# Eight PSUM banks assigned step by step, score blocks of three key chunks, and reordered first loads in an attention and feed-forward kernel

## The chip, the cores and the metric

The kernel runs on one core of one Trainium2 chip. TensorE does the matmuls and writes them to PSUM, which the kernel uses as eight banks; ACT, DVE and POOL are the other engines that compute. The metric is device microseconds of one execution, median over several, with the range beside it. Each timed execution also lists its mean granted TensorE clock (1.0 is full speed). A profile is one execution taken by the hardware profiler. Its span, from first to last instruction, is some 2 us shorter than the time of the same execution.

## The reference

```python
def _attn_ref(q, k, v, tau):            # 8 x 12 heads, 448 positions, 64 wide
    q_n = q / (norm(q) + 1e-06);  k_n = k / (norm(k) + 1e-06)
    scores = q_n @ k_n.T / tau
    attn = exp(scores - max);  attn /= sum(attn) + 1e-09
    return attn @ v
def _moe_ref(x, w1, w2, w3, w_out):     # x: 3584 x 768
    return ((x @ w1) * (x @ w2)) @ w3 @ w_out
```

## The kernel before

A scheduler in the kernel (class `Plan`) knows all steps, an assumed duration for each and the rings of buffers. It places the steps on the engines greedily in assumed time and then emits them, so the order on every engine is fixed when the kernel is built. Two heads make a pair; 48 pairs go through transposes (`tr`), scores, exponentials, the product with V (`av`), a transpose back (`tb`), and then the products of the feed-forward part ("fills": `a`, `b`, output groups, and at first the product w3 x w_out). Fills have the lowest rank and fill TensorE wherever attention leaves room. The parts that the change touches:

```python
psS = tile_pool(name="psS", bufs=2, space=PSUM)   # scores: 2 x 2 banks
psA = tile_pool(name="psA", bufs=1, space=PSUM)   # av: 1 bank
psT = tile_pool(name="psT", bufs=1, space=PSUM)   # tr and tb: 1 bank
psM = tile_pool(name="psM", bufs=2, space=PSUM)   # fills: 2 banks
...
def scores(pp, half):
    ...
    for c in (2 * half, 2 * half + 1):            # two key chunks in one block
        sc = psS.tile([128, 2, 512], FP32, tag="sc", name="sc")
        for hh in range(2):                       # two heads, 64 rows each, side by side
            kq = qks[pp][64 * hh:64 * hh + 64].rearrange("p t s -> p (t s)")
            nc.tensor.matmul(sc[:, hh, :S], kq[:, c * P:c * P + 128], kq[:, S:],
                             start=True, stop=True)
...
loads = ["w30", "wo0", "q0", "k0", "w31", "v0", "w32", "q1", "k1", "wo1", "w33",
         "w34", "v1", "q2", "wo2", "k2", "w10", "w20", "v2"]     # then q3 k3 v3 ...
...
for n in range(60):                               # warm-up matmuls while nothing else can run
    add(f"warm{n}", [("PE", 0.78 if n < 4 else 0.39)], 10000 + n, ..., until=11.0)
```

## Time and profile before

| what | value | how to read it |
|---|---|---|
| time, before the prediction | 401.64 us (401.2 to 402.2, 3 executions) | |
| span of the profile | 399.0 us | |
| TensorE busy | 98% | busy is not peak: gaps inside the stream count as busy |
| ACT, POOL, DVE busy | 62%, 62%, 55% | averages; POOL is at 91 to 96% from 40 to 240 us |
| mean granted clock | 0.995 | one fall to half speed near 16 us |

### The profile page before, as it was taken

To read this page: it belongs to the slowest core of one execution; us is meant where nothing else is said; L and a number is where in the kernel's file an instruction comes from. 1 tells how busy PE (TensorE), PEld (TensorE's weight loads), DVE (VectorE), ACT (ScalarE), POOL (GpSimd) and SP (SyncE) were. 2 spreads that over 40 slices of the span, in tenths; PEclk is the share of its full clock that TensorE was granted. 3 is DMA by queue.
4 is the path that set the end of the run, shared out by engine and by line. 5 is a ranking of instruction groups with operands and counts; after the bars stand their busy time and mean duration, and the time that the engine had idled before them with its cause. 6 is when DMAs were issued, how large, how long until landed. Compare 5 with 4: busy or idle time off the path is not lost.

```text
span 399.0 us, 9513 instructions
## 1 busy us (share of the span) xinstructions
PE 389.2 (98%) x4006; PEld 231.5 (58%) x4006; DVE 218.2 (55%) x490; ACT 247.7 (62%) x402; POOL 247.2 (62%) x260
## 2 busy tenths in 40 slices
PE   8799999999999999999999999999999999999996
PEld 4578665556555666555655556654665467555553
DVE  4986745685666946576566686643454244220210
ACT  3887667656777777678777777677467733223222
POOL 8779698899999999999999999960100000000000
PEclk9899999999999999999999999999999999999999
DMA  9999999073863758528485256200111004103005
GB/s 164 200 204 209 212 197 153 5 102 81 144 73 41 99 112 152 73 34 106 74 151 72 35 69 116 81 2 0 41 41 41 2 2 112 47 0 111 10 5 156
DMA packets 43691, 35.18 MB, mean 88 GB/s; under 512 B 3968, under 2 KB 37632, under 8 KB 43648
## 3 DMA queue, kind: packets, MB, share of 16 engines
q0 software_dynamic: 38368, 23.11, 42.3%
q1 hardware_dynamic: 4784, 11.07, 9.6%
q8 instruction: 31, 0.51, 0.5%
q10 hardware_dynamic: 496, 0.40, 0.3%
q14 instruction: 12, 0.10, 0.1%
HBM read 46.66 MB, written 11.01 MB: 145 GB/s over the span
## 4 chain that ended last, share of the span: by engine, by line
PE 74%; POOL 19%; DVE 3%; issue 2%; ACT 0%; ACTq 0%; POOLq 0%; DVEq 0%
PE ps_b L337 15%; PE ps_a L337 15%; PE ps_o L337 14%; PE ps_av L302 10%; PE sc L287 8%; POOL sq L231 8%; POOL nrm L257 8%; PE ps_w L337 5%; PE ps_tr L270 4%; PE ps_tb L324 2%; POOL v_sb L216 2%; PE ps_warm L437 2%; POOL raw L200 2%; DVE ss L237 1%; PE ps_w L350 1%
## 5 line engine op out<-in xcount | busy, mean ns | idle before, releaser
L293 ACT ACTIVATE expT<-sc 112x896 bf16<-112x896 f32 x192 | 165.9, 914 | 46.5 <-PE sc L287 46.4
L337 PEld LDWEIGHTS <-w_sb 128*128 128x128 bf16 x768 | 71.0, 98 | 60.3 <-issue 3.0
L257 POOL TENSOR_TENSOR nrm<-raw,rn 112x512 bf16<-112x512 bf16 x90 | 90.7, 1035 | 8.9 <-ACT rn L252 8.8
L231 POOL TENSOR_TENSOR sq<-raw 112x512 bf16<-112x512 bf16 x87 | 87.9, 1039 | 0.3
L337 PE MATMUL ps_a<-xT,w_sb 128*128 128x448 bf16 x384 | 83.1, 353 | 0.0
L337 PE MATMUL ps_b<-xT,w_sb 128*128 128x448 bf16 x384 | 83.0, 352 | 0.0
L337 PE MATMUL ps_o<-w_sb,abT 128*128 128x384 bf16 (+2 forms) x456 | 79.9, 323 | 0.0
L383 DVE TENSOR_TENSOR abT<-a_sb,ps_b 128x448 bf16<-128x448 bf16 x64 | 39.6, 619 | 69.2 <-PE ps_b L337 67.0
L237 DVE TENSOR_REDUCE ss<-sq 112x8 f32<-112x512 bf16 x96 | 63.4, 678 | 13.3 <-POOL sq L231 13.1
L302 PEld LDWEIGHTS <-expT 112*128 112x128 bf16 x1536 | 58.1, 98 | 19.0 <-issue 11.5
L302 PE MATMUL ps_av<-v_sb,expT 112*128 112x65 bf16 x1536 | 65.4, 194 | 0.0
L372 ACT CAST a_sb<-ps_a 128x448 bf16<-128x448 f32 x64 | 34.1, 532 | 45.4 <-PE ps_a L337 43.9
L337 PEld LDWEIGHTS <-abT 128*128 128x128 bf16 x456 | 41.8, 98 | 25.8 <-issue 2.2
L287 PE MATMUL sc<-qkT 64*128 64x448 bf16 x384 | 53.0, 354 | 0.0
L343 ACT COPY out_sb<-ps_o 128x384 f32<-128x384 f32 (+2 forms) x46 | 21.7, 471 | 40.1 <-PE ps_o L337 39.5
L315 DVE TENSOR_TENSOR osd<-ps_av,rs 128x256 bf16<-128x256 f32 x96 | 40.7, 424 | 3.3
L314 DVE RECIPROCAL rs<-ps_av 128x4 f32<-128x4 f32 x96 | 17.2, 179 | 42.1 <-PE ps_av L302 40.7
L278 DVE COPY qkT<-ps_tr 128x896 bf16<-128x896 bf16 x48 | 29.7, 619 | 6.7 <-PE ps_tr L270 6.6
L216 POOL COPY v_sb<-vraw 112x1536 bf16<-112x1536 bf16 x16 | 23.4, 1460 | 15.5 <-PE ps_av L302 15.5
L270 PE MATMUL ps_tr<-ident,nrm 112*128 112x112 bf16 x384 | 27.6, 215 | 1.2 <-DVE nrm L257 1.1
L270 PEld LDWEIGHTS <-nrm 112*128 112x128 bf16 x384 | 20.5, 98 | 13.6 <-issue 7.4
L331 DVE COPY xT<-ps_tb 128x448 bf16<-128x448 bf16 x48 | 18.5, 386 | 15.3 <-PE ps_tb L324 14.7
(37 smaller groups left out, 209.3 us busy)
## 6 DMA issues: line engine op xcount, KB each, us to landing
vraw<-in_v_dram POOLq DMA_DIRECT2D x16, 336.0 KB, 6.2
raw<-in_q_dram POOLq DMA_DIRECT2D x15, 336.0 KB, 5.1
raw<-in_k_dram POOLq DMA_DIRECT2D x15, 336.0 KB, 6.3
w_sb<-in_moe_w_dram POOLq DMA_DIRECT2D x2, 1536.0 KB, 26.3
out_dram<-out_sb SPq DMA_DIRECT2D x7, 336.0 KB, 2.8
out_dram<-out_sb SPq DMA_DIRECT2D x8, 288.0 KB, 2.9
out_dram<-out_sb SPq DMA_DIRECT2D x8, 240.0 KB, 2.8
w_sb<-in_moe_w_dram POOLq DMA_DIRECT2D x3, 512.0 KB, 15.4
```

Of the source, the lines that this page charges most:

```text
L216: nc.gpsimd.tensor_copy(v_tiles[g % NV][:, :, :, :D], vraws.pop(g))
L231: eng.tensor_mul(o, x, x)
L237: nc.vector.reduce_sum(sss[g][:, t, 2 * i:2 * i + 2, :], sqs.pop((g, i, t)), axis=AX.X)
L257: eng.tensor_mul(nrms[g][:, i, t].rearrange("p j h d -> p h j d"), raw_of(g, t, i), rns[g][:, t, 2 * i:2 * i + 2].to_broadcast([P, 2, NJ, D]))
L270: nc.tensor.transpose(ps[:, 1 - t, j * P:(j + 1) * P], n[:, i, t, j].rearrange("p h d -> p (h d)"), ident[:P, :P])
L287: nc.tensor.matmul(sc[:, hh, :S], kq[:, c * P:c * P + 128], kq[:, S:], start=True, stop=True)
L293: nc.scalar.activation(exps[pp][:, c], scs.pop((pp, c))[:P, :, :S], ACT.Exp, scale=1.0 / float(tau))
L302: nc.tensor.matmul(ps[:, m, :], exps[pp][:, c, hh, q0:q0 + 128], vt[:, 2 * i + hh, c, :], start=(c == 0), stop=(c == NJ - 1))
L315: nc.vector.tensor_mul(osds[pp][:, :, hh, :], ps[:, :, :D], rs.to_broadcast([128, NJ, D]))
L337: nc.tensor.matmul(o, l, r, start=(i == 0), stop=(i == len(pairs) - 1))
L372: nc.scalar.copy(a_sbs[b, fo], pms.pop(("a", b, fo))[:, :S])
L383: nc.vector.tensor_mul(abts[b // 2][:, fo, c0:c0 + S], a_sbs.pop((b, fo)), pms.pop(("b", b, fo))[:, :S])
```

## The change

Its intent is to take the banks out of fixed pools: one PSUM tile of eight banks is indexed, and the scheduler gives each TensorE step a free bank when it places it. Scores get three slots of two banks, so that a block can hold three key chunks and may reach from one pair into the next. The other short tiles may use the same six banks between score blocks. The first loads are reordered and those of the fourth group moved up. From the diff, with cuts and some comments added:

```diff
-    psS = ctx.enter_context(tc.tile_pool(name="psS", bufs=2, space=PSUM))
-    (psA, psT, psM likewise)
+    ps_all = psum.tile([128, 8, 512], FP32, name="ps")
...
-    loads = ["w30", "wo0", "q0", "k0", "w31", "v0", "w32", "q1", "k1", "wo1", "w33",
-             "w34", "v1", "q2", "wo2", "k2", "w10", "w20", "v2"]
+    loads = ["wo0", "q0", "k0", "w30", "w31", "w32", "v0", "q1", "k1", "wo1", "q2",
+             "w33", "v1", "w34", "wo2", "q3", "k2", "w10", "k3", "v3", "w20", "v2"]
...
+    PM = [(n,) for n in (7, 6, 5, 4, 3, 2)]          # banks for fills
+    SHORT = [(n,) for n in range(6)]                 # banks for tr, av, tb
+    while at < len(all_chunks):
+        n = 2 if all_chunks[at][0] < NFIRST else 3   # NFIRST = 6
+        blocks.append((at, all_chunks[at:at + n]))
+        at += n
...
-                     [("DVE", 0.1 + n * 0.00105), ("ACT", 0.2 + n * 0.00065)],
+                     [("DVE", 0.1 + n * 0.00105)] +
+                     ([("ACT", 0.2 + n * 0.00065)] if n > 128 else []),   # last output copy
```

More of the change, by code (lines that the diff above doesn't have):

```diff
@@ L38, in __init__ @@
         self.taken = {r: [] for r in rings}
+        self.owner, self.bank, self.reads = [None] * 8, {}, {}
     def given(self, name, time):
@@ L42, in given, with add @@
         self.where[name] = "DMA"
-    def add(self, name, on, rank, emit, after=(), takes=(), holds=(), kb=0, later=None,
-            until=None, slack=0.0, port=False, lead=None):
+    def add(self, name, on, rank, emit, after=(), takes=(), holds=(), reads=(), kb=0, later=None,
+            until=None, slack=0.0, port=False, lead=None, banks=()):
         self.steps[name] = dict(on=on, rank=rank, emit=emit, after=list(after), later=later,
-                                takes=list(takes), kb=kb, until=until, slack=slack, port=port, lead=lead or {})
+                                takes=list(takes), kb=kb, until=until, slack=slack, port=port, lead=lead or {},
+                                banks=banks)
+        for user, part in reads:
+            self.reads.setdefault(user, []).append((name, part))
         for key in holds:
@@ L76, in earliest @@
             t = max(t, self.port["POOL" if eng == "DVE" else "DVE"])
+        if st["banks"]:
+            when = [(self.opens(group, eng), group) for group in st["banks"]]
+            when = [x for x in when if x[0] is not None]
+            if not when:
+                return None
+            t = max(t, min(x[0] for x in when))
+            st["pick"] = next(group for at, group in when if at <= t)
         if st["kb"] and len(self.lanes) >= self.LANES:
@@ L79, in earliest, with readers, opens @@
         return None if st["until"] is not None and t > st["until"] else t
+    def readers(self, name, b):
+        return [r for r, x in self.reads.get(name, ()) if x is None or b in self.bank[name][x]]
+    def opens(self, group, eng):
+        at = [self.gone(self.owner[b], eng) if self.owner[b] else 0.0 for b in group]
+        return None if None in at else max(at)
     def order(self):
@@ L119, in order @@
                 self.taken[r].append(key)
+            if st["banks"]:
+                self.bank[n] = st["pick"]
+                for b in st["pick"]:
+                    self.owner[b] = ("bank", n, b)
+                    self.holders.setdefault(("bank", n, b), self.readers(n, b))
             for u in users.get(n, ()):
@@ L158 @@
     NP = B * NPAIR
+    NFIRST = 6
     QT = (0, 128, 256, S - 128)
@@ L173 @@
     opool = ctx.enter_context(tc.tile_pool(name="opool", bufs=3))
-    psS = ctx.enter_context(tc.tile_pool(name="psS", bufs=2, space=PSUM))
-    psA = ctx.enter_context(tc.tile_pool(name="psA", bufs=1, space=PSUM))
-    psT = ctx.enter_context(tc.tile_pool(name="psT", bufs=1, space=PSUM))
-    psM = ctx.enter_context(tc.tile_pool(name="psM", bufs=2, space=PSUM))
+    psum = ctx.enter_context(tc.tile_pool(name="psum", bufs=1, space=PSUM))
+    ps_all = psum.tile([128, 8, 512], FP32, name="ps")
     w1_sb = wpool.tile([128, KO1, DF], BF16, name="w1_sb")
@@ L262, with full, half @@
     qks, exps, osds, xts, pst, scs, pav = {}, {}, {}, {}, {}, {}, {}
+    def full(name):
+        return ps_all[:, plan.bank[name][0]]
+    def half(name):
+        return full(name).bitcast(BF16).rearrange("p (t n) -> p t n", t=2)
     def tr(pp):
@@ L266, in tr @@
         n = nrms[g]
-        ps = psT.tile([128, 2, 512], BF16, tag="tr", name="ps_tr")
+        ps = half(f"tr{pp}")
         for t in range(2):
@@ L278, in tr_copy, with scores @@
         nc.vector.tensor_copy(qks[pp], pst.pop(pp)[:, :, :S])
-    def scores(pp, half):
-        if half == 0:
-            exps[pp] = exp_pool.tile([P, NJ, 2, S], BF16, tag="exp", name="expT")
-        for c in (2 * half, 2 * half + 1):
-            sc = psS.tile([128, 2, 512], FP32, tag="sc", name="sc")
+    def scores(name, chunks):
+        for n, (pp, c) in enumerate(chunks):
+            if c == 0:
+                exps[pp] = exp_pool.tile([P, NJ, 2, S], BF16, tag="exp", name="expT")
+            b = plan.bank[name][2 * n]
+            sc = scs[pp, c] = ps_all[:, b:b + 2]
             for hh in range(2):
@@ L289, in scores @@
                     start=True, stop=True)
-            scs[pp, c] = sc
     def exp(pp, c):
@@ L298, in av @@
         vt = v_tiles[g % NV]
-        ps = psA.tile([128, NJ, D + 1], FP32, tag="av", name="ps_av")
+        ps = full(f"av{pp}.{hh}")[:, :NJ * (D + 1)].rearrange("p (m d) -> p m d", m=NJ)
         for m, q0 in enumerate(QT):
@@ L321, in trback @@
             xts[b] = xpool.tile([128, NPAIR, S], BF16, tag="xT", name="xT")
-        ps = psT.tile([128, 2, 512], BF16, tag="tr", name="ps_tb")
+        ps = half(f"tb{pp}")
         for m, q0 in enumerate(QT):
@@ L347, in w3t @@
     def w3t(fo):
-        ps = pms["w3t", fo] = psM.tile([128, KO2, 128], BF16, tag="pm", name="ps_w3")
+        ps = pms["w3t", fo] = half(f"w3t{fo}").rearrange("p t (k n) -> p (t k) n", n=128)
         for go in range(KO2):
@@ L355, in w34 @@
     def w34(fo, part, cols):
-        ps = pms["w34", fo, part] = psM.tile([128, 512], FP32, tag="pm", name="ps_w34")
+        ps = pms["w34", fo, part] = full(f"w34.{fo}.{part}")
         mm_group([(w3t_sb[:, go, fo * 128:(fo + 1) * 128], wo_sb[:, go, cols])
@@ L365, in a_group @@
     def a_group(b, fo):
-        ps = pms["a", b, fo] = psM.tile([128, 512], FP32, tag="pm", name="ps_a")
+        ps = pms["a", b, fo] = full(f"a{b}.{fo}")
         mm_group([(w1_sb[:, ko, fo * 128:(fo + 1) * 128], xts[b][:, ko, :])
@@ L374, in b_group @@
     def b_group(b, fo):
-        ps = pms["b", b, fo] = psM.tile([128, 512], FP32, tag="pm", name="ps_b")
+        ps = pms["b", b, fo] = full(f"b{b}.{fo}")
         mm_group([(w2_sb[:, ko, fo * 128:(fo + 1) * 128], xts[b][:, ko, :])
@@ L407, in out_group @@
     def out_group(bb, ch, cols):
-        ps = pms["o", bb, ch, cols.start] = psM.tile([128, 512], FP32, tag="pm", name="ps_o")
+        ps = pms["o", bb, ch, cols.start] = full(f"o{bb}.{ch}.{cols.start}")
         mm_group([(abts[bb][:, fo, ch * 128:(ch + 1) * 128], w34_sb[:, fo, cols])
@@ L432, with warm @@
     ident = const.tile([128, 128], BF16)
-    def warm():
-        ps = psM.tile([128, 512], FP32, tag="pm", name="ps_warm")
+    def warm(n):
+        ps = full(f"warm{n}")
         for _ in range(2):
@@ L444 @@
     plan = Plan(
-        rings=dict(sc=2, av=1, tr=1, pm=2, raw=3, vraw=2, vt=NV, sq=6, nrm=3, qkT=2, osd=2,
+        rings=dict(raw=3, vraw=2, vt=NV, sq=6, nrm=3, qkT=2, osd=2,
                    exp=3, xT=2, a_sb=KO2, big=1, out_sb=3),
@@ L458 @@
         weights[f"w3{n}"] = (w3_sb, moe_w3, part, every)
-    loads = ["w30", "wo0", "q0", "k0", "w31", "v0", "w32", "q1", "k1", "wo1", "w33",
-             "w34", "v1", "q2", "wo2", "k2", "w10", "w20", "v2"]
-    for g in range(3, NG):
+    loads = ["wo0", "q0", "k0", "w30", "w31", "w32", "v0", "q1", "k1", "wo1", "q2",
+             "w33", "v1", "w34", "wo2", "q3", "k2", "w10", "k3", "v3", "w20", "v2"]
+    for g in range(4, NG):
         loads += [f"q{g}", f"k{g}", f"v{g}"]
@@ L536 @@
             [f"v{g}", "ones"], [("vt", ("vt", g))], [("vraw", g)],
-            slack=0.8 if g > 0 else 0.0)
+            slack=0.8 if g > 0 else 0.0, port=True)
+    PM = [(n,) for n in (7, 6, 5, 4, 3, 2)]
+    SHORT = [(n,) for n in range(6)]
+    all_chunks = [(p, c) for p in range(NP) for c in range(NJ)]
+    blocks, at = [], 0
+    while at < len(all_chunks):
+        n = 2 if all_chunks[at][0] < NFIRST else 3
+        blocks.append((at, all_chunks[at:at + n]))
+        at += n
+    for nb, (at, ch) in enumerate(blocks):
+        ps = sorted({p for p, _ in ch})
+        slots = [b for n in range(len(ch)) for b in (2 * ((at + n) % 3), 2 * ((at + n) % 3) + 1)]
+        add(f"sc{nb}", [("PE", 0.205 + 0.187 * len(ch))], ch[0][0] + 0.25 * ch[0][1] - 1,
+            lambda e, nb=nb, ch=ch: scores(f"sc{nb}", ch),
+            [f"ev{p}" for p in ps] + ([f"sc{nb - 1}"] if nb else []),
+            [("exp", ("exp", p)) for p, c in ch if c == 0], [("qkT", p) for p in ps],
+            banks=[tuple(slots)])
+        for n, (p, c) in enumerate(ch):
+            add(f"exp{p}.{c}", [("ACT", 0.82)], p + 0.25 * c - 1,
+                lambda e, p=p, c=c: exp(p, c),
+                [f"sc{nb}"] + ([f"exp{p}.{c - 1}"] if c else [f"exp{p - 1}.{NJ - 1}"] if p else []),
+                reads=[(f"sc{nb}", slice(2 * n, 2 * n + 2))],
+                lead={f"sc{nb}": 0.187 * (len(ch) - 1 - n)})
     for p in range(NP):
@@ L544 @@
             [f"scale{p}.0", f"scale{p}.1", "ident"] + ([f"tr{p - 1}"] if last else []),
-            [("tr", ("tr", p)), ("qkT", ("qkT", p))], [("nrm", g)],
-            slack=0.3 if g > 2 else 0.0)
+            [("qkT", ("qkT", p))], [("nrm", g)],
+            slack=0.3 if g > 2 else 0.0, banks=SHORT)
         add(f"ev{p}", [("DVE", 0.54)], p - 1.1, lambda e, p=p: tr_copy(p), [f"tr{p}"],
-            holds=[("tr", p)])
-        for h in range(2):
-            add(f"sc{p}.{h}", [("PE", 0.58)], p + 0.5 * h - 1, lambda e, p=p, h=h: scores(p, h),
-                [f"ev{p}"] + ([f"sc{p}.0"] if h else [f"sc{p - 1}.1"] if last else []),
-                [("sc", ("sc", p, 2 * h)), ("sc", ("sc", p, 2 * h + 1))]
-                + ([] if h else [("exp", ("exp", p))]), [("qkT", p)])
-            for c in (2 * h, 2 * h + 1):
-                add(f"exp{p}.{c}", [("ACT", 0.82)], p + 0.25 * c - 1,
-                    lambda e, p=p, c=c: exp(p, c),
-                    [f"sc{p}.{h}"] + ([f"exp{p}.{c - 1}"] if c else []), holds=[("sc", p, c)])
+            reads=[(f"tr{p}", None)])
         for h in range(2):
@@ L561 @@
                 + ([f"av{p}.0"] if h else [f"av{p - 1}.1"] if last else []),
-                [("av", ("av", p, h))] + ([] if h else [("osd", ("osd", p))]),
-                [("exp", p), ("vt", g)])
+                [] if h else [("osd", ("osd", p))], [("exp", p), ("vt", g)], banks=SHORT)
             add(f"an{p}.{h}", [("DVE", 0.62)], p + 0.5 * h - 0.5,
-                lambda e, p=p, h=h: av_norm(p, h), [f"av{p}.{h}"], holds=[("av", p, h)])
+                lambda e, p=p, h=h: av_norm(p, h), [f"av{p}.{h}"], reads=[(f"av{p}.{h}", None)])
         add(f"tb{p}", [("PE", 0.235)], p + 1, lambda e, p=p: trback(p),
             [f"an{p}.0", f"an{p}.1"] + ([f"tb{p - 1}"] if last else []),
-            [("tr", ("tb", p))] + ([] if blk else [("xT", ("xT", b))]), [("osd", p)])
+            [] if blk else [("xT", ("xT", b))], [("osd", p)], banks=SHORT)
         add(f"xt{p}", [("DVE", 0.31)], p - 0.2, lambda e, p=p: tb_copy(p), [f"tb{p}"],
-            holds=[("tb", p)])
+            reads=[(f"tb{p}", None)])
     line = []
@@ L582, in fill @@
     def fill(nm, cost, em, after, on, em2, takes=(), holds=(), after2=(), holds2=(), lead=None):
-        add(nm, [("PE", cost)], 1000 + len(line), em, after, [("pm", ("pm", nm))] + list(takes),
-            holds, later=line[-1] if line else None, lead=lead)
-        add(nm + ".c", on, -50, em2, [nm] + list(after2), holds=[("pm", nm)] + list(holds2))
+        add(nm, [("PE", cost)], 1000 + len(line), em, after, list(takes),
+            holds, later=line[-1] if line else None, lead=lead, banks=PM)
+        add(nm + ".c", on, -50, em2, [nm] + list(after2), holds=list(holds2), reads=[(nm, None)])
         line.append(nm)
@@ L634 @@
     for n in range(60):
-        add(f"warm{n}", [("PE", 0.78 if n < 4 else 0.39)], 10000 + n, lambda e: warm(),
-            takes=[("pm", ("warm", n))], later=f"warm{n - 1}" if n else None, until=11.0)
+        add(f"warm{n}", [("PE", 0.78 if n < 4 else 0.39)], 10000 + n, lambda e, n=n: warm(n),
+            banks=PM, later=f"warm{n - 1}" if n else None, until=11.0)
     for n, e in plan.order():
```

## The prediction

> **What bounds the kernel now.** I read the page's first table, then the table of stretches, then the waits of TensorE, then TensorE's instructions in order of time, and last the head of the chain of waits. Table of engines, kernel before:
>
> ```profile
> PE 389.2 (98%) x4006; PEld 231.5 (58%) x4006; DVE 218.2 (55%) x490; ACT 247.7 (62%) x402; POOL 247.2 (62%) x260
> ```
>
> TensorE is busy all the time, no other engine over 62%. Busy does not mean useful, so the next question is where it is idle. Stretches (columns: stretch, length, then busy us and count for PE, PEld, DVE, ACT, POOL, then granted clock, DMA share, GB/s):
>
> ```profile
> 0.00:8.00 8.00, 6.74 (x28) 3.15 (x29) 3.03 (x7) 3.83 (x10) 6.87 (x15) 1.00 0.93 157
> 8.00:16.00 8.00, 5.38 (x54) 3.06 (x50) 6.96 (x9) 5.88 (x16) 7.22 (x11) 1.00 1.29 201
> 16.00:20.00 4.00, 3.51 (x42) 3.21 (x44) 3.64 (x8) 2.68 (x4) 2.05 (x3) 0.57 1.50 195
> 20.00:40.00 20.00, 19.34 (x291) 15.80 (x287) 15.10 (x38) 16.18 (x30) 17.34 (x19) 1.00 1.27 206
> 40.00:160.00 120.00, 120.00 (x1334) 70.94 (x1331) 78.81 (x178) 83.64 (x133) 109.45 (x111) 1.00 0.75 114
> 160.00:240.00 80.00, 79.03 (x892) 45.70 (x891) 53.42 (x121) 58.07 (x92) 76.92 (x79) 1.00 0.54 77
> ```
>
> From 27 us to the end of the matmuls at 395 us TensorE stands still for about 1 us; all other idling is in the first 27 us. Its waits, whole list:
>
> ```profile
> PE ps_w L337 <- DVE w3t_sb L345: 1.9, 2, 1.5
> PE ps_warm L437 <- DVE warm_sb L431: 1.3, 1, 1.3
> PE ps_tr L270 <- DVE nrm L257: 1.1, 1, 1.1
> PE ps_tb L324 <- DVE qkT L278: 1.0, 2, 0.5
> PE ps_w L337 <- DVE w_sb L345: 0.7, 1, 0.7
> ```
>
> So more PSUM cannot buy much by removing waits: only the last two of the five come from a full PSUM (1.0 us: a transposed output shares its one bank with the q/k transposes; 0.7 us: two banks for the weight products). What is left is the price of the work itself. TensorE's instructions in order of time (start, length, what):
>
> ```profile
> 104.19 1.30 PE L337 MATMUL ps_b<-xT,w_sb 128*128 128x448 bf16 x6
> 105.32 0.68 PE L302 MATMUL ps_av<-v_sb,expT 112*128 112x65 bf16 x16
> 105.93 0.55 PE L287 MATMUL sc<-qkT 64*128 64x448 bf16 x4
> 106.41 0.57 PE L270 MATMUL ps_tr<-ident,nrm 112*128 112x112 bf16 x8
> 106.82 1.30 PE L337 MATMUL ps_a<-xT,w_sb 128*128 128x448 bf16 x6
> 107.95 0.39 PE L324 MATMUL ps_tb<-ident,osd 128*128 128x128 bf16 x4
> 108.18 1.30 PE L337 MATMUL ps_b<-xT,w_sb 128*128 128x448 bf16 x6
> 109.41 0.55 PE L287 MATMUL sc<-qkT 64*128 64x448 bf16 x4
> 109.89 0.69 PE L302 MATMUL ps_av<-v_sb,expT 112*128 112x65 bf16 x16
> 110.42 0.92 PE L337 MATMUL ps_a<-xT,w_sb 128*128 128x448 bf16 x4
> ```
>
> The printed lengths overlap; the difference of two starts is what a block costs. The b block before av takes 1.13 us (0.189 a matmul), but the b block before a score block takes 109.41 - 108.18 = 1.23. An av block before a takes 0.53, before scores 105.93 - 105.32 = 0.61. A score block takes 0.48, although its four matmuls run two by two (64 rows each) and two times 0.19 is 0.38. So every score block pays about 0.095 us on entry and 0.095 on exit, 0.19 us together, whatever stands beside it. The reader is to see this: it is invisible as a wait and is counted as busy.
>
> **What the Trainium skill says.** "TensorEngine Tiling (Array Packing)", section Tiling Modes, Key Properties: "Changing tiling mode (not just tile) drains the TensorE". The scores are the only 64-row tiles in a stream of full-height ones (112 or 128 rows), and the trace agrees, with 0.19 us a visit. "TensorE: Matmul & The Clock Gate", Part 1: the array starts at half clock, is released after some 3.4 us of activity and can fall back after idling. The trace agrees: the warm-up matmuls start 0.37 us apart up to about 5.8 us and 0.19 apart after, and in the stretch 16 to 20 us, after two waits of 1.5 and 1.1 us, the granted clock was 0.57. "Perfetto Trace Analysis", section Matmul Optimizations, advises to use all eight PSUM banks; the kernel before holds all eight already, but in fixed shares (4 scores, 1 av, 1 transposes, 2 rest), and its TensorE hardly waits for them.
>
> **The change part by part.**
>
> Score blocks. Before: 96 blocks of two key chunks (384 matmuls of the row "sc", four each), and in the order of instructions no two touch. After: the order of the changed kernel shows 12 blocks of four matmuls (first six pairs) and 56 of six, none touching: 68. Removed: 28 visits x 0.19 = 5.3 us. TensorE is the path from 27 us on, so this comes off the end unless a wait takes its place. The third chunk streams at 0.19-0.2 us as before, so I count 5.1 us. Products, transposes, exponentials and copies are the same in number (16 weight and output copies change between DVE and ACT).
>
> Banks. The 1.0 us for tb and the 0.7 us (with its ramp about 0.9) for the weight products go, as tb, tr and av may use any of six banks, and fills six. Removed: up to 1.9 us; the second is part of the start, below.
>
> First loads. Up to the fifth transfer the bytes are the same and only their order differs: wo0, q0, k0, w30, w31 in place of w30, wo0, q0, k0, w31. At the 0.2 MB/us of the stretch table, q0 and k0 land 256 KB or 1.3 us earlier and the first w3 slice 3 us later. The first product of weights, which filled 7.7 to 9.7 us, goes behind the first scores. In its place stand 14 more warm-up matmuls: 7.67 + 14 x 0.189 = 10.3 us, and only then the first q/k transpose (9.74 before), although its input would be there at 8.8. I followed both orders with the durations above: first scores 11.9 (11.4 before), then the wait for the w3 copy behind four sums on DVE, about 1.2 us (1.5 before), second scores 14.9 (14.8), second transpose 15.6 (16.4, and at full clock, I think), a wait of 1.3 for a w3 copy that ACT does after two exponentials, third transpose 18.4, both av blocks done at 21.5 against 21.4 for the same work. The later 0.9 us wait falls away. Net of the start: -0.8 us, uncertain by 1.5. The fourth group's earlier load gives POOL work before 60 us; TensorE is not short of work there, so it is worth nothing by itself.
>
> End. The last 128 columns are copied by DVE beside the 256 on ACT: the copy of 0.27 us started 0.4 late after its matmuls, gain 0.2 us.
>
> Sum: -5.1 (visits) -1.0 (tb waits) -0.8 (start) -0.2 (end) = -7.1 us, on the condition that nothing new waits. The scheduler fixes all orders from assumed durations, and those were short for ACT (it assumes 0.82 us for an exponential; the row has 0.91, 0.86 apart when back to back) and for DVE sums (0.60 against 0.68). A block of six needs all three slots: TensorE's third pair waits for the last exponential of the block before. I allow +0.8 us for new waits. Result: 401.6 - 6.3 = 395.3 us.
>
> **The rivals.**
>
> (1) Score blocks wait for ACT. For it: ACT sits behind other work, and slots are now also lent to tr, av and tb. Against it: by the new order the work on TensorE between the starts of two six-blocks is mostly 4 to 6 us and never under about 3.2, while three exponentials are 2.6 us; ACT is at 62%. If one block in four waits 0.3 us, it costs 4 us: 399.
>
> (2) POOL becomes the path. For it: POOL is busy 186 of 200 us between 40 and 240, and the chain of waits runs over its squares and scalings from 118 to 203 us:
>
> ```profile
> by line: PE ps_b L337 14.8%; PE ps_a L337 14.7%; PE ps_o L337 13.7%; PE ps_av L302 9.6%; PE sc L287 8.0%; POOL sq L231 7.9%; POOL nrm L257 7.5%; PE ps_w L337 4.9%; PE ps_tr L270 3.9%; issue 2.3%; PE ps_tb L324 2.1%; POOL v_sb L216 1.8%; PE
> ```
>
> Against it: in that stretch TensorE stood still twice for half a microsecond, and only since DVE's copy, queued behind a sum that waited for POOL, held the one transpose bank; there are now others. A batch needs about 33 us of POOL (24 passes of 1.04, two copies of 1.46, six issues of 0.8) and about 44 us of TensorE (355 us from 40 to 395 us for eight), and, counted in the trace, at 180 us four batches of attention were done and 2.8 of the first product: TensorE has a reserve. If I am wrong, the 3 us saved before 203 us are lost: 398.
>
> (3) The start goes much better or worse: a second fall of the clock costs 1.5 us more; a start without it and without the waits for w3 copies saves 3 in place of 0.8: 393 to 397.
>
> **Range and chances.** The visits are certain to within 0.5 us; start and new waits have about 2 us of spread each way, somewhat more upwards. 2% is 8.0 us, that is 393.6: it needs everything to go well with no new wait. Hence 395.3, range 392.0 to 398.8; faster by over 2% 0.22, within 0.76, slower 0.02.
>
> **What would show it.** The row of scores again with 384 matmuls but in blocks of six, starts about 0.67 us apart from what follows; TensorE's waits for DVE's qkT copy gone; idling outside the first 25 us under 1.5 us; both first av blocks done near 21.5 us; a last matmul near 388.5 in place of 395. Waits of the scores for ACT of over 2 us in sum, or an entry cost that grows with the block, would make it wrong.

## The result, and the profile after

The changed kernel takes 395.40 us (395.08 to 395.83, 4 executions), the kernel before 401.42 us (400.97 to 402.20, 4 executions). The ratio is 0.9849, with a 95% interval of 0.983 to 0.987. Ratios here are the mean time of one kernel's fast runs over that of the other's of the same rounds, so not quite the ratio of the medians quoted. By the 2% threshold the two count as the same; the difference is clear of the noise all the same.

The first table of the page of the changed kernel (line numbers have moved: scores are L316, transposes L298, av L330, all fills L365; every PSUM tile is now called ps):

```profile
PE 384.1 (98%) x4018; PEld 231.9 (59%) x4018; DVE 211.3 (54%) x486; ACT 245.6 (62%) x406; POOL 247.3 (63%) x260
```

TensorE does 12 matmuls more (warm-ups) in 5.1 us less and is as busy as before: it is the same bound, with cheaper work. The stretches, columns as before:

```profile
16.00:20.00 4.00, 2.82 (x43) 2.37 (x44) 2.91 (x6) 3.85 (x5) 2.96 (x4) 1.00 1.47 196
20.00:40.00 20.00, 18.60 (x300) 15.11 (x297) 13.76 (x36) 16.91 (x30) 17.84 (x20) 1.00 1.31 204
40.00:160.00 120.00, 120.00 (x1319) 72.77 (x1315) 78.15 (x177) 81.36 (x138) 114.29 (x116) 1.00 0.73 115
160.00:240.00 80.00, 79.69 (x863) 47.27 (x863) 49.34 (x112) 54.64 (x87) 77.21 (x79) 1.00 0.59 91
```

The clock in the first row is 1.00, where the kernel before had 0.57. The second row is the surprise: TensorE is busy for 18.6 of 20 us there, before it was 19.3. All waits of TensorE in the changed kernel:

```profile
PE ps L365 <- DVE w3t_sb L373: 1.3, 1, 1.3
PE ps L465 <- DVE warm_sb L459: 1.3, 1, 1.3
PE ps L365 <- ACT w3t_sb L371: 1.1, 1, 1.1
PE ps L316 <- DVE qkT L306: 0.4, 1, 0.4
PE ps L298 <- POOL nrm L279: 0.4, 1, 0.4
PE ps L352 <- ACT expT L321: 0.4, 1, 0.4
PE ps L330 <- POOL v_sb L238: 0.3, 1, 0.3
PE ps L330 <- DVE qkT L306: 0.2, 1, 0.2
```

The two waits of before that came from a full PSUM (tb for DVE's qkT copy, the weight product for DVE's w_sb copy) are gone. Five short ones stand in their place, all but the last of them between 19 and 40 us. TensorE's instructions in order of time, a stretch like the one shown of before:

```profile
104.49 0.39 PE L352 MATMUL ps<-ident,osd 128*128 128x128 bf16 x4
104.72 1.30 PE L365 MATMUL ps<-xT,w_sb 128*128 128x448 bf16 x6
105.95 0.74 PE L316 MATMUL ps<-qkT 64*128 64x448 bf16 x6
106.62 1.31 PE L365 MATMUL ps<-xT,w_sb 128*128 128x448 bf16 x6
107.77 0.56 PE L298 MATMUL ps<-ident,nrm 112*128 112x112 bf16 x8
```

The group before the scores still takes 105.95 - 104.72 = 1.23 us, that is 0.095 more than its stream, and the block of six takes 106.62 - 105.95 = 0.67 us, three streams of 0.19 and about 0.1 on exit. So the price of a visit is what it was; there are fewer visits.

**Where the time went.** I took the start of every matmul from each trace and split the time from the first to the last one into four parts: streaming (each form of matmul at its median start-to-start interval, a score pair at 0.191 us), visits to the scores (a visit is one block of score matmuls among other work; 0.195 us each in the table, while the medians block by block are 0.096 on entry and 0.101 on exit, 0.197 together), warm-ups, and what is left over, that is waits and slow clock. "After 42 us" is the part of the leftover that lies after the start. All in us, from the profiled executions. (A recount with visits at 0.197 and medians to the nanosecond gave 359.1 of streaming in every row and 0.6 to 0.9 less in the next to last column; the differences between rows stay within 0.3.)

| kernel | first to last matmul | streaming | visits | warm-ups | waits and slow clock | of it after 42 us |
|---|---|---|---|---|---|---|
| before | 393.7 | 358.4 | 18.7 | 8.6 | 7.9 | 2.4 |
| changed | 388.3 | 358.4 | 13.2 | 9.5 | 7.2 | 1.6 |
| run 1, blocks of two | 395.3 | 358.4 | 18.7 | 10.5 | 7.6 | 3.0 |
| run 2, old loads | 390.3 | 358.4 | 13.2 | 8.8 | 9.9 | 3.3 |
| run 3, banks only | 394.9 | 358.4 | 18.7 | 9.1 | 8.6 | 2.2 |
| run 4, one height of tile | 383.4 | 358.5 | 0 | 9.6 | 15.3 | 8.9 |
| run 7, all blocks of three | 391.1 | 358.4 | 12.4 | 9.8 | 10.4 | 5.3 |
| run 11, other assumed durations | 399.7 | 358.4 | 13.2 | 10.0 | 18.1 | 13.7 |

Between before and changed, the difference is 5.4 us, and the visits alone account for 5.5. The start costs 1.0 us (warm-ups plus waits before 42 us: 8.6 + 5.5 before, 9.5 + 5.6 after) and the later waits give 0.8 back. After the last matmul starts, the span goes on for 4.1 us before and 4.4 after.

### The profile page after: what moved, and what is told of

Same layout as the page of the kernel before. It is cut to its first block, busy times and chain, and to the rows that moved or that the text cites. A ratio compares the mean times of both kernels' runs of the same rounds, so it can differ in the third digit from the quotient of the medians.

```text
span 394.0 us, 9648 instructions
## 1 busy us (share of the span) xinstructions
PE 384.1 (98%) x4018; PEld 231.9 (59%) x4018; DVE 211.3 (54%) x486; ACT 245.6 (62%) x406; POOL 247.3 (63%) x260
## 4 chain that ended last, share of the span: by engine, by line
PE 77%; POOL 14%; DMA 5%; issue 2%; ACT 1%; DVE 1%; POOLq 0%; DVEq 0%
PE ps L365 52%; PE ps L330 10%; PE ps L316 9%; POOL sq L253 5%; POOL nrm L279 5%; PE ps L298 4%; DMA raw<-in_k_dram 3%; PE ps L352 2%; DMA wo_sb<-in_moe_w_out_dram 2%; POOL raw L222 1%; POOL v_sb L238 1%; ACT expT L321 1%; POOL vraw L229 1%; DVE qkT L306 0%; POOL w_sb L241 0%
## 5 line engine op out<-in xcount | busy, mean ns | idle before, releaser
L321 ACT ACTIVATE expT<-ps 112x896 bf16<-112x896 f32 x192 | 165.9, 921 | 26.6 <-PE ps L316 26.6
L365 PE MATMUL ps<-xT,w_sb 128*128 128x448 bf16 x768 | 161.7, 353 | 0.0
L365 PEld LDWEIGHTS <-w_sb 128*128 128x128 bf16 x768 | 68.9, 98 | 65.2 <-issue 12.6
L365 PE MATMUL ps<-w_sb,abT 128*128 128x384 bf16 (+2 forms) x456 | 80.1, 324 | 0.0
L411 DVE TENSOR_TENSOR abT<-a_sb,ps 128x448 bf16<-128x448 bf16 x64 | 39.6, 619 | 69.6 <-PE ps L365 64.6
L400 ACT CAST a_sb<-ps 128x448 bf16<-128x448 f32 x64 | 34.0, 532 | 60.3 <-PE ps L365 60.1
L365 PEld LDWEIGHTS <-abT 128*128 128x128 bf16 x456 | 41.6, 98 | 31.4 <-issue 7.4
L330 PEld LDWEIGHTS <-expT 112*128 112x128 bf16 x1536 | 54.8, 98 | 7.5 <-issue 2.1
L330 PE MATMUL ps<-v_sb,expT 112*128 112x65 bf16 x1536 | 57.0, 194 | 0.6 <-POOL v_sb L238 0.3
L316 PE MATMUL ps<-qkT 64*128 64x448 bf16 x384 | 48.8, 353 | 0.5 <-DVE qkT L306 0.4
L343 DVE TENSOR_TENSOR osd<-ps,rs 128x256 bf16<-128x256 f32 x96 | 40.8, 425 | 3.3
L306 DVE COPY qkT<-ps 128x896 bf16<-128x896 bf16 x48 | 29.7, 619 | 11.7 <-PE ps L298 11.6
L359 DVE COPY xT<-ps 128x448 bf16<-128x448 bf16 x48 | 18.6, 386 | 25.0 <-PE ps L352 21.9
L316 PEld LDWEIGHTS <-qkT 64*128 64x128 bf16 x384 | 13.5, 94 | 27.9 <-issue 21.5
L298 PE MATMUL ps<-ident,nrm 112*128 112x112 bf16 x384 | 27.0, 213 | 0.4 <-POOL nrm L279 0.4
L365 PE MATMUL ps<-wo_sb,w3t_sb 128*128 128x192 bf16 (+1 forms) x192 | 23.6, 273 | 2.5 <-DVE w3t_sb L373 1.3
## 6 DMA issues: line engine op xcount, KB each, us to landing
w_sb<-in_moe_w_dram POOLq DMA_DIRECT2D x3, 512.0 KB, 16.1
```

The costliest lines, as they stand in the source:

```text
L298: nc.tensor.transpose(ps[:, 1 - t, j * P:(j + 1) * P], n[:, i, t, j].rearrange("p h d -> p (h d)"), ident[:P, :P])
L306: nc.vector.tensor_copy(qks[pp], pst.pop(pp)[:, :, :S])
L321: nc.scalar.activation(exps[pp][:, c], scs.pop((pp, c))[:P, :, :S], ACT.Exp, scale=1.0 / float(tau))
L330: nc.tensor.matmul(ps[:, m, :], exps[pp][:, c, hh, q0:q0 + 128], vt[:, 2 * i + hh, c, :], start=(c == 0), stop=(c == NJ - 1))
L343: nc.vector.tensor_mul(osds[pp][:, :, hh, :], ps[:, :, :D], rs.to_broadcast([128, NJ, D]))
L365: nc.tensor.matmul(o, l, r, start=(i == 0), stop=(i == len(pairs) - 1))
```

## The experiments

Twelve kernels ran. The theory is the visit theory of the prediction: each change from full-height tiles to the 64-row score tiles and back costs about 0.2 us. Its rivals are that the free banks made the gain, or that the reordered loads did. All results are correct but that of run 4.

**Run 1: blocks of two throughout.** `NFIRST = 6` becomes `NFIRST = 48`; banks and loads stay.

> The changed kernel with score blocks of two chunks throughout (96 visits in place of 68); eight banks and first loads as in the changed kernel. Visit theory: in both traces a block of four matmuls costs 0.58 us from start of its entry gap to the next block, a block of six 0.77, so a visit costs 0.20 us and the 28 visits come back: 395.4 + 5.6 = 401.0 us, 400 to 402. Bank theory (the gain came from waits that the free banks removed): stays at 395 to 397 us. Load theory (the reordered loads made it): 395 to 397 us as well.

Measured: 402.54 us (402.3 to 402.7), ratio to before 1.0042. The whole gain is gone, and a little more than I expected. In the table, 5.5 us of the 7.0 us between this kernel and the changed one are visits; 1.0 are warm-ups at half clock (the release from half speed came later in this execution) and 0.4 waits. The bank and load theories, which both asked for 397 or less, fall.

**Run 2: old loads.** The list of loads is that of before, the rest as changed.

> The changed kernel with the first loads in the order of before; banks and blocks of three chunks stay. Visit theory: nothing of size, 394.5 to 396.5 us; from the count of finished work the changed kernel was about 0.6 us behind the kernel before at 42 us, so the old order may even be 0.6 us better: 394.8. Load theory: loses 2 us or more, 397.5 us or over.

Measured: 397.66 us (396.84, 397.52, 397.80, 402.55), ratio 0.9953 with a wide interval of 0.988 to 1.003. By its number this falls to the load theory, and the visit theory's "nothing of size" was wrong. The list of executions tells more than the median: their mean clocks are 0.998, 0.994, 0.989 and 0.981, in the order of their times. The same stretch as above, in this kernel's profiled execution:

```profile
16.00:20.00 4.00, 2.89 (x25) 1.72 (x23) 3.55 (x5) 2.83 (x5) 2.90 (x4) 0.50 1.45 197
```

Half clock all through, where the changed kernel has 1.00. Even the execution with 0.998 is 1.4 us over the changed kernel's median, and the table has 1.7 us more waits after 42 us: the scheduler, starting from other loads, laid out another order for everything.

**Run 3: banks only.** Old loads and `NFIRST = 48`.

> Old loads and blocks of two chunks: of the change only the free assignment of banks is left. Visit theory: as the kernel before less the waits for full banks (about 1.5 us of waits in its trace, some replaced by others): 400 to 401.5 us. Bank theory: 397 us or less.

Measured: 402.45 us (402.09 to 406.34), ratio 1.0062, interval 1.001 to 1.011. The free assignment of banks by itself gains nothing and loses about half a per cent; it was even a little worse than the visit theory allowed. Its clocks are 0.996, 0.995, 0.989 and 0.983. Runs 1 and 3 differ in the loads alone and have the same median.

**Run 4: one height of tile.** Wrong result. Each score matmul uses all 128 rows and half the columns:

```diff
-                kq = qks[pp][64 * hh:64 * hh + 64].rearrange("p t s -> p (t s)")
+                kq = qks[pp].rearrange("p t s -> p (t s)")
...
-                    sc[:, hh, :S], kq[:, c * P:c * P + 128], kq[:, S:],
+                    sc[:, hh, :S // 2], kq[:, c * P:c * P + 128], kq[:, S:S + S // 2],
```

and the exponential reads each written half twice. Orders and banks are those of the changed kernel.

> Wrong result on purpose: each score matmul uses all 128 rows (both heads summed) and half the columns, 224 in place of 448, and the exponential reads each half twice, so TensorE streams as long as before (two matmuls of 0.095 us one after the other against two of 0.19 side by side), all orders and banks stay, but the tile height never changes. If the 0.20 us a visit is the change of tile height: 68 x 0.20 = 13.6 us go, 381.8 us, at most 3 us of new waits, so 381 to 385, and the gaps at entry and exit of a score block fall to zero in the trace. If the gap is a wait for the banks, for ACT or for the weights whatever the height: 394 to 396 us and the gaps stay.

Measured: 391.27 us (390.64 to 393.75), ratio 0.9773. The mechanism is settled by three lines of its trace, TensorE in order of time:

```profile
102.58 1.30 PE L367 MATMUL ps<-xT,w_sb 128*128 128x448 bf16 x6
103.72 0.74 PE L316 MATMUL ps<-qkT 128*128 128x224 bf16 x6
104.29 1.30 PE L367 MATMUL ps<-xT,w_sb 128*128 128x448 bf16 x6
```

The group before the scores takes 1.14 us in place of 1.23, and the six score matmuls take 0.57, six times 0.095 and nothing more. In 63 of the 68 visits the entry gap is 0 or 1 ns; the other five stand behind waits. So the price is that of changing to the 64-row tiles, not of waiting for ACT, banks or weights. The edit also ends the running of two matmuls side by side and halves the columns that each writes; which of these carries the price, the height alone or the pairing with it, was not told apart. But of the 13.2 us that this takes from TensorE only 4.9 arrive at its last matmul, and my 381 to 385 was wrong. The table shows the other 8.3 nearly whole: 8.1 us more of waits, most of them after 42 us. The chain of waits of this run points to who took over:

```profile
by line: PE ps L367 33.6%; POOL nrm L279 16.1%; POOL sq L253 15.2%; PE ps L332 5.5%; issue 4.7%; PE ps L316 4.2%; POOL v_sb L238 3.7%; POOL raw L222 3.5%; DMA raw<-in_k_dram 3.2%; PE ps L298 2.1%; DMA wo_sb<-in_moe_w_out_dram 1.8%; POOL vra
```

POOL's squares and scalings hold 31% of the span; in the changed kernel the same two have 10.5%. That is the second rival of the prediction, which does not bite at 395 us and does when TensorE gets another 13 us cheaper, at least in orders that were laid out for the dearer scores. Whether orders laid out anew would do better was not tried.

**Run 5: the changed kernel again**, as a control on the chip of runs 6 to 8.

> The changed kernel itself, as a control on the same chip and in the same rounds as the next three. All theories: 395 to 396 us, ratio to before 0.985.

Measured: 395.83 us (395.69, 395.70, 395.95 and 398.73), ratio 0.9855. The one slow execution happened to be the profiled one, with a clock of 0.991, the others have 0.998. Its stretches show what happened:

```profile
8.00:16.00 8.00, 5.70 (x45) 3.26 (x45) 5.42 (x9) 4.85 (x10) 4.36 (x8) 0.89 1.24 204
16.00:20.00 4.00, 2.90 (x30) 2.00 (x29) 2.17 (x3) 3.00 (x8) 2.32 (x3) 0.79 1.47 196
20.00:40.00 20.00, 18.96 (x276) 15.23 (x275) 14.00 (x34) 16.64 (x31) 16.70 (x18) 0.91 1.32 204
40.00:160.00 120.00, 119.97 (x1333) 73.22 (x1331) 78.86 (x178) 82.11 (x135) 113.62 (x116) 1.00 0.74 115
```

The clock fell to half twice, from 14.3 to 17.7 and from 21.1 to 24.5 us. Same code, same orders, 3 us longer.

**Run 6: fills in two fixed banks.** `PM` becomes `[(7,), (6,)]`.

> Blocks of three chunks and new loads stay; the fills (weight products, a, b and output groups) may use two fixed banks only, as before, in place of six. Bank theory in its weak form (the free choice of banks removes waits): waits of TensorE for evacuations come back, 397 us or more. Visit theory: the loan of score banks to fills is worth nothing, 394.8 to 396.3 us.

Measured: 395.42 us (395.09, 395.38, 395.45 and 397.50 at a clock of 0.996), ratio 0.9838. Nothing is lost. The order of instructions on TensorE is identical to the changed kernel's. Lending the score banks to the fills is worth nothing; what the shared banks are good for is the third score slot.

**Run 7: blocks of three from the first pair on.** `NFIRST = 0`.

> Blocks of three chunks from the first pair on: 64 visits in place of 68. Visit theory: 4 x 0.20 = 0.8 us less, 394.6 us, but the first exponentials and so the first av come later and the start may take it back: 394 to 396.5.

Measured: 398.81 us (398.58 to 399.49), ratio 0.9917, with clocks of 0.998 to 1.000. The visits fell by 0.8 us as they should, and the kernel is 3 us slower. The table has the reason: 5.3 us of waits after 42 us in place of 1.6. The largest single one is TensorE standing still before an av block near 113 us, as DVE's qkT copy for its bank came late. Work and engines are the same. The greedy order came out worse.

**Run 8: fewer warm-ups.** `until=11.0` becomes `until=8.0`.

> 28 warm-up matmuls in place of 42, so the first q/k transpose need not wait for them: in the trace of the changed kernel its input is ready at 8.39 us and it starts at 9.49. If the start follows the first transpose: 0.5 to 1.2 us less, 394.3 to 395.0 us. If the start is set by the loads and the copies of w3 after it: same as the control within 0.3 us. If the clock falls back: 1 us worse.

Measured: 397.21 us (397.01 to 398.04), ratio 0.9876, clocks 0.991 in the profile and 0.986 in all three timed executions. The last of the three expectations holds: the clock fell in each of them. The first transpose started at 9.40 us in place of 9.49, so there was nothing to win there, because the release from half speed came later in this execution and the 28 matmuls took as long as 36.

**Runs 9 and 10: dummy matmuls against the falls.** In run 9 the changed kernel gets six dummy matmuls before the product that waits for the first w3 copy, and six before the second; run 10 does this on top of run 8, with five before the first scores. Their output goes to the bank of the step that follows.

```diff
+    dummies = {"w34.0.0": 6, "w34.1.0": 6}
     for n, e in plan.order():
+        for _ in range(dummies.get(n, 0)):
+            nc.tensor.matmul(full(n)[:, :S], warm_sb[:, :128], warm_sb[:, :S], start=True, stop=True)
```

> The changed kernel with six dummy matmuls (result overwritten by the product that follows) in each of its two long waits for a w3 copy, near 12 and 16 us; the order is else the same. Clock theory (what differs between executions, 395.1 to 398.7 us, are falls of the granted clock in the first 40 us after those waits): no execution under a mean clock of 0.998, all within 395.0 to 396.0 us, median 395.3. If the spread has another cause: median the same, single executions over 397 us remain. If dummies delay the work: 395.8 to 397.

> The kernel with 28 warm-up matmuls, which had a clock of 0.986 and 397.0 to 397.3 us in its timed executions, with five dummies before the first scores and six in each of the two waits. Clock theory: the clock stays at 0.998 to 1.000 and the time falls by 1.5 to 2.5 us, to 394.8 to 395.6. If 397 us came from somewhere else: stays at 397.

Measured: run 9 397.03 us (396.51 to 398.49, clocks 0.996 to 1.000), ratio 0.9882; run 10 398.86 us (396.74 to 401.28, clocks 0.987 to 1.000), ratio 0.9909. Both are failures of the edit. Two waits of run 9:

```profile
PE ps L683 <- DVE w3t_sb L373: 1.2, 1, 1.2
PE ps L683 <- ACT w3t_sb L371: 1.1, 1, 1.1
```

L683 are the dummies themselves. The scheduler had given the product the very bank that the w3 transpose before it had filled, so the dummies waited for the same copy and then stood in the way. In run 10 the dummies before the first scores waited 3.1 us for DVE's qkT copy.

**Run 11: assumed durations nearer to the measured ones** (exponential 0.82 to 0.87, sums 0.60 to 0.66, three DVE copies and products 0.05 or 0.06 more). Nothing else changes.

> The changed kernel with durations in its scheduler nearer to the measured ones (exponential 0.87 for 0.82, sums 0.66 for 0.60, copies and b products 0.05 to 0.06 more); work, banks and block sizes are the same, only the orders move. If the waits of TensorE that are left after 42 us (1.3 to 4.8 us in the runs so far) come from durations set too short: they fall under 1 us, 394 to 395.5. If each new order draws its own waits, as with blocks of three from the start: anywhere from 394.5 to 399.

Measured: 407.22 us (406.65 to 408.05), ratio 1.013. This is the worst kernel, with the same work and the same number of visits. The table has 13.7 us of waits and slow clock after 42 us; some 3 of them (an estimate, from the starts of the matmuls) are a fall of the clock from 196.3 to 203.1 us. The first cluster of waits, near 98 us, shows how they arise:

```profile
98.70 0.62 DVE L306 COPY qkT<-ps 128x896 bf16<-128x896 bf16 x1
98.81 0.35 PE L316 MATMUL ps<-qkT 64*128 64x448 bf16 x1 [0.15 <-DVE xT L359]
...
99.24 1.86 DVE L259 TENSOR_REDUCE ss<-sq 112x8 f32<-112x512 bf16 x3
99.26 0.34 ACT L271 ACTIVATE rt<-ss,tiny 112x48 f32<-112x48 f32 x1
99.37 0.72 PE L316 MATMUL ps<-qkT 64*128 64x448 bf16 x5 [0.22 <-DVE qkT L306]
```

The scores sit in TensorE's order right behind a transpose whose copy DVE has not finished, with no fill put in between, and the exponential behind them waits for four small ACT steps. The second of my two readings holds: each new order draws its own waits, and closer durations do not make it a better one.

**Run 12: the dummies mended.** Five in each wait, into bank 6, which nothing uses until 18 us.

> The dummies of the ninth run mended: five in each wait, into a bank that nothing uses until 18 us, so that they fill the wait for the w3 copy and do not wait for it themselves. Clock theory: no execution under a mean clock of 0.998 and none over 396.2 us (the changed kernel had 2 in 8 at 397.5 and 398.7), median 395.2, ratio to before 0.983 to 0.985. If the falls of the clock have another cause than these waits: single executions at 397 or more with a clock under 0.997 remain.

Measured: 395.57 us (395.17 to 396.28, 6 executions), clocks 0.997 to 1.000, ratio 0.9846. No execution is over 396.3 us, while the twelve of the same order without dummies (changed kernel, run 5 and run 6) reach to 398.7. The edit does what it should: the two waits shrink from 1.3 and 1.1 us to 0.4 and 0.2. It misses my line in small points (one at 396.28 with a clock of 0.999, one clock of 0.997, a median 0.4 us above the forecast). The median is no better than the changed kernel's. Six executions without a deep fall support the theory that the idle waits bring the falls, but with 2 in 12 slow ones for the same order (the changed kernel, run 5 and run 6) they do not prove it.

**What the clock makes of all this.** The kernel before ran 22 times beside runs 9 to 12. (The mean clock counts the fall after the last matmul too: run 1's 0.998 is that alone.) Nine of these executions had a clock of 0.991 and took 402.2 to 403.4 us, twelve had 0.993 to 0.996 and took 400.7 to 402.0, and one had 0.999 and took 400.78. The changed orders (changed kernel, run 5, run 6) had 0.998 or more in 10 of 12, with 395.1 to 396.0 us. At a full clock the changed kernel takes about 395.5 us. For the kernel before there is one such execution, at 400.8; the two groups lie 1.55 us apart in the mean (402.88 and 401.32), and one step more would put it near 399.8, an estimate. So the two are 4.3 to 5.3 apart there, near the 5.5 of the visits but not shown to be exactly that. The rest of the 6.0 us between the medians goes to the kernel before losing its clock for 3.4 or 6.8 us in nearly every execution and the changed one seldom. The new loads and the longer warm-up go with that: run 8, with 14 warm-up matmuls fewer, fell in all four executions, and runs 2 and 3, with the old loads and six fewer, show it too (one of eight executions at 0.998 or more, against four of four in run 1).

The traces tell when the clock falls. In all 14 profiles the stretches of the clock, from the first release to full speed up to the last matmul, are multiples of 3.41 us. Cut each profile into windows of that length from its first release on, and add up the time in which TensorE is idle: at full clock ten windows were idle for 1.63 to 2.38 us, and each was followed by a fall; the other 1558 were idle for 1.33 us at most, and none was. In the kernel before, parts of the waits of 1.5 and 1.1 us share one window (2.10 us idle, 12.7 to 16.1 us); in the changed kernel's profile the waits of 1.3 and 1.1 us lie in two. The first release came anywhere from 4.0 to 7.1 us, so which waits share a window differs between executions of the same code. In run 12's profile no window is idle for over 0.5 us. This is read from the profiles after the fact, and no run was made to test it.

No experiment beat the changed kernel: runs 6 and 12 are equal to it within their spread.

## Why the prediction was right

The time was forecast as 395.3 us and is 395.4. The sum agrees better than its terms do. Of the signs it named, the blocks of six came 0.67 us apart and TensorE idled for 1.0 us after the first 25. But two waits for the qkT copy remain (0.6 us, not those of tb), and the last matmul started at 389.6 us, not near 388.5.

- **Visits.** Forecast 5.1 us, measured 5.5 (28 times 0.197). I had charged the third chunk with up to 0.2 us; it streams in 0.19. Runs 1 and 4 show the mechanism from both sides: with 28 visits more the gain is gone, with none the gaps are gone.
- **Full banks.** The two tb waits (1.0 us) and the weight product's wait went as forecast. Run 3 shows that this is worth nothing net.
- **New waits.** I allowed 0.8 us. Together with the tb waits this made 0.2 us of gain; measured are 0.8 after 42 us. Right in sign, but the term was no more than a guess: runs 7 and 11 show that an order of the same work can cost 4 or 12 us there. Here the prediction was lucky.
- **Start: the step that failed.** I forecast 0.8 us of gain. Up to the two first av blocks it went better than forecast (the block after them starts at 20.8 us, before at 21.3; forecast 21.5 and 21.4), in part by luck: the first transpose started at 9.49 us and not at 10.3, as the release from half speed came at 4.16 us in this execution (5.84 in the profile before). In run 6, with the same order, it came at 6.38 us and the transpose started at 10.59. Then the 0.9 us wait for the w_sb copy fell away. What I did not follow was the stretch from 20 to 40 us: three new waits of 0.4 us each, for an exponential, POOL's scaling and DVE's qkT copy, turn it, with smaller ones, into a loss of 1.0 us in the profiled execution. I had also written "at full clock, I think" in passing. The clock had an effect of its own: in most executions it does stay at full speed, which is worth 0.7 to 1.7 us in the medians (6.0 less the 5.3 or 4.3 above, an estimate).
- **End.** Forecast 0.2 us of gain. The last copy did start earlier, but the span did not keep it:

```profile
394.75 0.37 ACT L343 COPY out_sb<-ps_o 128x256 f32<-128x256 f32 x1 [0.35 <-PE ps_o L337]
395.15 0.34 ACTq L396 DMA_DIRECT2D out_dram<-out_sb  x1
395.53 0.27 ACT L343 COPY out_sb<-ps_o 128x128 f32<-128x128 f32 x1 [0.41 <-PE ps_o L337]
```

```profile
389.39 0.37 ACT L371 COPY out_sb<-ps 128x256 f32<-128x256 f32 x1 [0.35 <-PE ps L365]
389.79 0.82 ACTq L424 DMA_DIRECT2D out_dram<-out_sb  x2
389.89 0.29 DVE L373 COPY out_sb<-ps 128x128 f32<-128x128 f32 x1 [9.78 <-PE ps L365]
```

  These are the last copies in order of time, before and after. The last copy starts 0.59 us after the last matmul's start before (394.94) and 0.31 after (389.58), but the span ends 4.1 us after that start before and 4.4 us after. Other profiles with the new end have 4.1 to 4.5 us. The packets in the traces show where it went: the last one of the output lands 2.46 us after that matmul's start before and 2.42 after, so only 0.04 of the 0.28 us reached the last landing. What follows, the semaphores that close the kernel, takes 1.63 us before and 1.99 after; why stays open.
- **Rivals.** ACT did not hold the scores back: no wait of L316 for ACT is in the list, and the one of 0.4 us for an exponential is at a transpose back (L352). POOL did not become the path at 395 us; run 4 shows that it does further down. The clock rival was named with the right size (1.5 us a fall). It was given to chance; the start's waits set how likely a fall is, and chance, the moment of the first release, still has its part.

## What to carry to other kernels

The 64-row matmuls cost 0.1 us on entry and 0.1 on exit here, which is counted as busy and appears in no list of waits; subtract the starts of neighbouring blocks to find it, and batch such matmuls as far as PSUM allows. In a statically ordered kernel, judge a change of order by several orders: two with the same work differed here by 12 us (some 3 of them a fall of the clock), so a gain of 1 or 2 us from a reordering may be luck. Before explaining 2 or 3 us between executions, sort them by granted clock.

## What the Trainium skill lacked or had wrong

- "TensorEngine Tiling (Array Packing)", Key Properties, says that a change of tiling mode drains TensorE and gives no figure. Here it is 0.096 us on entry and 0.101 on exit, 0.197 us a visit, and the gaps are gone where full-height tiles are kept (run 4).
- "TensorE: Matmul & The Clock Gate", section HAM oscillation, puts the rule as no idle gaps over about 3.4 us. The section after it, on a second failure mode, says that frequent short idling brings falls too, but gives no figure for how much. In the kernel before, the clock fell at 16.1 us, during the second of two waits of 1.5 and 1.1 us with work between them, and stayed down for 3.4 us; in other executions falls lasted 6.8 us (run 2) and 10.2 us (run 10). What separated falls from none in the 14 profiles is the idle time summed over a window: 1.63 us or more against 1.33 or less. The page's window of 3413 ns agrees: the lengths of all falls recorded before the last matmul are multiples of 3.41 us.
- "Perfetto Trace Analysis", section Matmul Optimizations, advises to use all eight banks. The kernel before uses all eight too, so the advice itself was not tested. Free use of all of them without larger blocks was worth nothing (run 3, ratio 1.006), nor was lending more banks to the fills (run 6, 395.42 us). No page says that the third score slot is what pays.
